# A second batch's scores kept in a copy instead of computed twice, and the order of work around them

## The chip, the cores and the metric

The kernel runs on one core of one Trainium2 chip. A core has TensorE (called PE in the rows: it multiplies, and transposes by multiplying with an identity), VectorE (DVE), ScalarE (ACT), GpSimd (POOL) and SyncE (SP), which issues DMA transfers here. Each engine works through its own list of instructions in order. Products land in PSUM, eight banks of 128 x 512 floats; everything else lives in SBUF. The metric is the time of one execution on the device in microseconds.

## The reference

Eight batches (B) with eight heads (H), 512 tokens (S) of width 64 (D), and 32 states for each head. Tokens read the states and states read the tokens, by one softmax each over the transposed scores. Both results go through one feed-forward layer with a hard gate. In all there are 8 x 544 = 4352 rows of width 512, and 2048 hidden columns.

```
scores = scale * np.matmul(x, state.transpose(0, 1, 3, 2))
a = softmax(scores);  xread = np.matmul(a, state)
scores2 = scale * np.matmul(state, x.transpose(0, 1, 3, 2))
a2 = softmax(scores2); sread = np.matmul(a2, x)
x = concat([xread, sread], axis=2), heads side by side   # 4352 rows
h = x @ w_in
g = h * np.clip(h + 3.0, 0.0, 6.0) / 6.0
return g @ w_out
```

## The kernel before

For the tokens, reading the states and multiplying by w_in are joined: `wprime` makes w' = states x w_in for a batch, and the first product is w' times the softmax weights, turned ("aT"). The hidden columns of a batch are worked in 16 steps of 128, four to a chunk; step n of the program has a first product (`first`, L831, into one of two banks `ps_h`), a gate (ACT L881, DVE L883), a split of the gated values into a high and a low part (ACT L246, DVE L247: `g_hi`, `g_lo`) and, two steps later, a second product into four banks `acc` (`second`, also L831). A product of split numbers is three matmuls. The first four steps work in plain fp32 instead (L860 and L900). In the trace a plain matmul has two records, so an x8 in an order below is an x16 there. The states' own rows come last, as a ninth batch.

Attention of a batch b, in the names of the code:

- `scores_by_columns` (its product is in `all_heads`, L458) multiplies states and tokens into two banks `ps_s`. `tokens_by_columns` makes the tokens' softmax of them (DVE L674 transposes the bank into SBUF; then L565 to L582, L680, and the split `aT_hi`, `aT_lo`). `states` makes the states' softmax of the same scores (DVE max L693, scaling L695, ACT exp L697, reciprocal L700 and L702). For the first two batches the tokens' half is needed early and the states' half is put off: its score product is made once more later (name "L"), so that the two banks are not held meanwhile. The first batch's tokens' half works by rows instead (`tokens_by_rows`), so it needs column scores only once, for the states.
- The states' weights are then laid out for reading: for batch 0 by PE (L731), for batch 1 by a DVE transpose (L745) and 32 small DMAs on SP (L752), for later batches by L758 and 16 DMAs (L766).
- `tokens_read` (64 small matmul records, L796; DVE L805) is the states' reading of the tokens. It rides on a later score product: in one entry with it, right behind. Ahead of its matmuls stands the turn of the result before (L791, one transpose by PE).
- `load_state` fetches the states of a later batch by four DMAs (L382) and turns them on DVE (L389) into `stT`. `load_turned` fetches tokens ahead (L445, sixteen DMAs for a batch), `load_x` the tokens to be read (L413). Weights come by L303; ACT (L308, L312) and DVE (L316, L320, L327) convert them, and w_out is split by ACT L352 and DVE L354. They pass through staging buffers, tag "raw", that the sixteen L445 use later too. Results leave by L935.

The order on each engine is made by a small list scheduler (`Plan`). Each operation is given a cost in us, a rank and what it reads and writes. `T` adds one for PE, `V` for DVE, `S_` for ACT, `Q` for SP; among those that can start about now, the lowest rank goes first. The program is then issued in that order on each engine. The ranks of the early weights, of the second batch and of the put-off halves are a table of numbers near the end (`weights`, `LATE`, `LATE_STEP`, `rank1`).

Of the kernel before, what the change touches and what calls it, by code (L numbers as in the profile page):

```python
# [10 lines left out]
F32 = mybir.dt.float32  # L11
# [3 lines left out]
ALU = mybir.AluOpType  # L15
# [134 lines left out]
def tile_state_attention_then_hardswish_ffn(  # L150
# [218 lines left out]
    def load_state(b, rank, after=()):  # L369
# [15 lines left out]
        if b < TURNED:  # L385
# [3 lines left out]
        V(0.22, rank + 1.0, lambda: nc.vector.transpose(  # L389
            get(("stT", b), lambda: att.tile([P, P], F32, name="stT")), made[key]), [key], [("stT", b)])  # L390
# [84 lines left out]
    def wprime(b, parts, rank, banks=None, after=()):  # L475
# [12 lines left out]
        at = T(0.26 + sum(0.95 * w[3] / CH for w in work), rank, run,  # L488
               [("stT", b)] + [k for c, f0, f1, *_ in work for k in w_in_keys(c * FPC + f0, c * FPC + f1)],
               [k for w in work for k in w[5]], after)  # L490
# [178 lines left out]
    def tokens_by_columns(b, rank, ps):  # L669

        hi_lo = weights_of(b)
        for g in range(NG):
# [12 lines left out]

    def states(b, rank, ps):

        r_key = ("r2", (b, 0))
        r2 = lambda: get(r_key, lambda: small.tile([P, NG], F32, name="r2", bufs=2))
        for g in range(NG):  # L690
# [3 lines left out]
                n2(), bank(ps[g]), axis=AX.X, op=ALU.max), [ps[g]], [n_key])  # L694
# [3 lines left out]
                tmp(e_key), bank(ps[g]), AF.Exp, bias=n2(), scale=SCALE, accum_out=r2()[:, g : g + 1]),  # L698
                [ps[g], n_key], [e_key, (*r_key, g)])
# [75 lines left out]
    def tokens_read(b, tag="ps_s"):  # L775
# [13 lines left out]
        def read():  # L789
            for key in last_key:  # L790
                nc.tensor.transpose(bank(pr)[:, place(1)], tmp(key)[:, : NG * D], ident)  # L791
# [19 lines left out]
        return 1.0 + 0.11 * len(last), read, [*t_key, *x_parts, *last_key], [pr], then  # L811

    def tokens_read_alone(b, rank, after=()):
        cost, read, reads, writes, then = tokens_read(b)
        T(cost + 0.2, rank, read, reads, writes, after)
        then()
# [158 lines left out]
    for seg, (b, c0, c1) in enumerate(segments):  # L975
# [11 lines left out]
        (0, "in", 0, 1, ("early0", 0, 0), -5.67, -19.58), (1, "in", 1, 1, ("early0", 0, 1), -3.50, -8.04),  # L987
        (2, "in", 2, 2, ("early1", 0), 0.77, -7.20), (-0.34, "out", 0, 1, ("raw", ("out", 0)), -2.50, -6.17),
        (-0.90, "out", 1, 1, ("raw", ("out", 1)), -0.36, -1.02), (0.55, "out", 2, 1, ("raw", ("out", 2)), 2.49, -3.00),
        (5.05, "out", 3, 1, ("early3", 0, 0), 2.13, -1.44),  # L990
# [73 lines left out]
    at(6, lambda: [f(4.88 + 0.2 * k) for k, f in enumerate(late_halves)])  # L1064
# [31 lines left out]
    take_in(0, -14.82, (), accs)  # L1096
    tokens_by_rows(0, lambda k: -2.51, lambda k: (), accs)
    load_x(1, -3.76)
    for n in range(len(steps)):
# [7 lines left out]
        elif b < 2 and n % FPC == 0:  # L1107
            ends = wp_parts[b, c][1:] + [FPC]
            for f0, f1 in zip(wp_parts[b, c], ends):
                weights_until(n + f1 - 1)  # L1110
                s = n - 3 + f0
                wprime(b, [(c, f0, f1)], s + 0.41 if n else (11.83, -6.49, 0.01)[f0],
                       ["acc2", "acc3"] if n == 0 and f1 < 3 else None,
                       [first_of[s]] if n >= 8 else ())
        if n == 0:
            take_in(1, -0.41, [scores_at[0]])
# [41 lines left out]
```

## Time and profile before

| | us |
|---|---|
| median of 3 runs | 663.51 (663.09 to 663.54) |
| the profiled execution | 663.73 |
| its span | 661.9 |
| PE busy | 651.0 (98%) |
| DVE busy | 420.2 (63%) |
| ACT busy | 310.8 (47%) |

The span runs from the first to the last thing that the profiler recorded; 1.83 us of the execution's time lie around it. A timeline row has the start, the busy time, engine, line, operation, output and inputs, the tile (rows x columns of PE used), the operand's shape and the number of records; in brackets stand idle time just before it and what ended that. A row of a DMA queue (SPq) gives the time that the queue took to issue, not the landing. A row of windows has the stretch, its length, then busy time and instructions of PE, PE's weight loads, DVE, ACT and POOL, the granted clock, the DMA share and GB/s. One matmul of 512 columns is recorded as busy longer than the distance to the next, so costs are read from start to start.

### The profile page before, as it was taken

The page shows a single profiled execution, that of the slowest core. Times are in us where ns is not written, and L with a number is a line of the kernel's source. Part 1 is how long each engine was busy: PE and PEld are TensorE (multiplying, and loading weights), DVE is VectorE, ACT ScalarE, POOL GpSimd, SP SyncE. Part 2 cuts the span into 40 slices and gives each one's busy share as a digit, 9 for nine tenths or more (in the row PEclk, how much of TensorE's full clock was granted, in tenths as well). Part 3 has the DMA queues.
Part 4 walks back from the last instruction along what each step waited for, and adds up shares of the span by engine and source line. Part 5 has one row for each costly group of instructions (what it writes and reads, how often), then busy time and mean ns, then how long its engine had stood idle before and what let it go on. Part 6 is the DMA issues. An engine that isn't in the chain of part 4 may idle for free.

```text
span 661.9 us, 9937 instructions
## 1 busy us (share of the span) xinstructions
PE 651.0 (98%) x3950; PEld 502.5 (76%) x3950; DVE 420.2 (63%) x697; ACT 310.8 (47%) x520; POOL 1.0 (0%) x7
## 2 busy tenths in 40 slices
PE   8899999999999999999999999999999999999997
PEld 7446777777686877787877877787778788788896
DVE  4998999885846945953677356944585353543542
ACT  5888777543523543443444343633343343333542
POOL 0000000000000000000000000000000000000000
PEclk9999999999999999999999999999999999999999
DMA  9807452415052243314050503132131001000101
GB/s 272 308 0 214 133 181 81 96 27 139 13 109 74 34 70 94 66 26 70 1 132 9 84 5 109 24 52 44 65 65 24 8 1 65 1 0 1 64 0 33
DMA packets 130894, 46.26 MB, mean 70 GB/s; under 512 B 119200, under 2 KB 121248, under 8 KB 130720
## 3 DMA queue, kind: packets, MB, share of 16 engines
q1 hardware_dynamic: 130704, 45.37, 27.9%
q8 instruction: 31, 0.51, 0.3%
q10 hardware_dynamic: 144, 0.26, 0.1%
q14 instruction: 15, 0.12, 0.1%
HBM read 33.03 MB, written 8.91 MB: 63 GB/s over the span
## 4 chain that ended last, share of the span: by engine, by line
PE 92%; DVE 3%; SPq 2%; DMA 2%; issue 0%; ACT 0%; DVEq 0%; ACTq 0%
PE acc L831 53%; PE ps_h L831 28%; PE ps_s L458 4%; PE acc L900 2%; DMA st_raw<-in_state_dram 2%; PE ps_h L458 2%; SPq L752 2%; PE ps_h L796 1%; PE ps_h L860 1%; PE ps_s L611 1%; SPq L382 0%; DVE g L883 0%; PE acc L546 0%; DVE g_lo L247 0%; DVE s L571 0%
## 5 line engine op out<-in xcount | busy, mean ns | idle before, releaser
L831 PE MATMUL acc<-w_out_hi,g_hi 128*128 128x512 f32 x528 | 209.1, 396 | 0.0
L831 PE MATMUL acc<-w_out_hi,g_lo 128*128 128x512 f32 x528 | 205.6, 389 | 0.3 <-DVE g_lo L247 0.3
L831 PE MATMUL acc<-w_out_lo,g_hi 128*128 128x512 f32 x528 | 205.9, 390 | 0.0
L881 ACT ACTIVATE g<-ps_h,three 128x512 f32<-128x512 f32 (+1 forms) x144 | 95.6, 664 | 212.5 <-PE ps_h L831 208.2
L883 DVE SCALAR_TENSOR_TENSOR g<-g,ps_h 128x512 f32<-128x512 f32 (+1 forms) x144 | 94.5, 657 | 136.9 <-ACT g L881 136.2
L831 PEld LDWEIGHTS acc<-w_out_hi,g_hi 128*128 128x128 f32 x528 | 99.1, 188 | 35.5 <-issue 13.4
L246 ACT CAST g_hi<-g 128x512 fp32r<-128x512 f32 (+1 forms) x140 | 83.3, 595 | 85.1 <-DVE g L883 84.8
L247 DVE TENSOR_TENSOR g_lo<-g,g_hi 128x512 fp32r<-128x512 f32 (+1 forms) x140 | 92.0, 657 | 46.2 <-ACT g_hi L246 43.8
L831 PEld LDWEIGHTS acc<-w_out_hi,g_lo 128*128 128x128 f32 x528 | 99.1, 188 | 21.8 <-DVE g_lo L247 0.8
L831 PEld LDWEIGHTS acc<-w_out_lo,g_hi 128*128 128x128 f32 x528 | 99.2, 188 | 18.9
L831 PE MATMUL ps_h<-aT_hi,wp_hi 128*128 128x512 f32 (+1 forms) x248 | 90.7, 366 | 0.0
L831 PE MATMUL ps_h<-aT_hi,wp_lo 128*128 128x512 f32 (+1 forms) x248 | 89.7, 362 | 0.0
L831 PE MATMUL ps_h<-aT_lo,wp_hi 128*128 128x512 f32 (+1 forms) x248 | 89.7, 362 | 0.0
L831 PEld LDWEIGHTS ps_h<-aT_hi,wp_hi 128*128 128x128 f32 x248 | 46.8, 189 | 8.5 <-DVE wp_lo L247 0.3
L831 PEld LDWEIGHTS ps_h<-aT_lo,wp_hi 128*128 128x128 f32 x248 | 46.8, 189 | 8.2 <-DVE early L316 0.3
L831 PEld LDWEIGHTS ps_h<-aT_hi,wp_lo 128*128 128x128 f32 x248 | 46.8, 189 | 7.3
L831 PE MATMUL ps_h<-aT_hi,wp 128*128 128x512 f32 x128 | 44.6, 389 | 0.0
L831 PEld LDWEIGHTS ps_h<-aT_hi,wp 128*128 128x128 f32 x128 | 24.0, 188 | 5.0
L831 PE MATMUL ps_h<-aT_lo,wp 128*128 128x512 f32 x64 | 24.9, 389 | 0.0
L458 PE MATMUL ps_s<-w_in,stT 64*32 64x512 f32 (+1 forms) x384 | 24.0, 557 | 0.0
L537 DVE STREAM_TRANSPOSE tmp<-raw 128x512 f32<-128x512 f32 x24 | 16.4, 699 | 6.5 <-DMA raw<-in_x_dram 6.5
L247 DVE TENSOR_TENSOR wp_lo<-ps_s,wp_hi 128x512 fp32r<-128x512 f32 (+1 forms) x34 | 19.8, 621 | 0.3 <-ACT wp_hi L246 0.3
(119 smaller groups left out, 506.4 us busy)
## 6 DMA issues: line engine op xcount, KB each, us to landing
out_dram<-ot SPq DMA_DIRECT2D x8, 1024.0 KB, 4.5
early<-in_moe_w_in_dram SPq DMA_DIRECT2D x7, 1024.0 KB, 7.1
xb<-in_x_dram SPq DMA_DIRECT2D x28, 256.0 KB, 4.1
raw<-in_x_dram SPq DMA_DIRECT2D x96, 64.0 KB, 2.1
early<-in_moe_w_out_dram SPq DMA_DIRECT2D x4, 1024.0 KB, 5.5
raw<-in_moe_w_out_dram SPq DMA_DIRECT2D x7, 512.0 KB, 4.4
raw<-raw SPq DMA_DIRECT2D x96, 32.0 KB, 2.0
early<-in_moe_w_in_dram SPq DMA_DIRECT2D x2, 512.0 KB, 5.3
```

The costliest lines, as they stand in the source:

```text
L246: S_(cost, rank, lambda: nc.scalar.copy(hi(), src()), reads, [writes[0]])
L247: V(cost, rank, lambda: nc.vector.tensor_tensor(lo(), src(), hi().bitcast(F32), op=ALU.subtract), [*reads, writes[0]], [writes[1]])
L458: nc.tensor.matmul(out[u][cols, :], made["stT", b][rows, cols], moving(q)[rows], start=True, stop=True,)
L537: V(0.7, rank, lambda q=q, key=key: nc.vector.transpose(xT(b, q), made[key][:, q % 2]), [(*key, q % 2, u, k) for u in range(2) for k in ra ...
L611: nc.tensor.matmul(out[:, j, q], xT(b, q)[:, js], apart[:, q], start=True, stop=True,)
L752: nc.sync.dma_start(dst[:, :, q], src[:, :, c])
L796: nc.tensor.matmul(bank(pr)[cols, u * D : (u + 1) * D], e2T(b, u)[:, j * P + q * NS : j * P + (q + 1) * NS], x_tile(b, True)[:, NG * q + u ...
L831: nc.tensor.matmul(ps, l, r, start=start and k == 0, stop=stop and k == n - 1)
L860: nc.tensor.matmul(bank(ps), made["wp_32", (b, k)][:, g, fs], a_first(g), start=g == 0, stop=g == NG - 1)
L881: S_(cost + 0.05, rank, lambda: nc.scalar.activation(g(), bank(ps)[:, :width], AF.Relu, bias=three), [ps], [g_key])
L883: V(cost, rank, lambda: nc.vector.scalar_tensor_tensor(g(), g(), 6.0, bank(ps)[:, :width], op0=ALU.min, op1=ALU.mult), [ps], [g_key])
L900: nc.tensor.matmul(bank(acc), made["g_hi", n][:, js], plain_out[i][1](), start=opens, stop=closes)
```

## The change

- The second score product of batch 1 goes. Right after the first one, ACT copies its two banks into SBUF (`kept_key`, L686 of the new file), and the put-off `states(1)` takes max and exp from the copies. The copies and the DVE transposes (L690) read the same banks; in the new order the transposes wait for ACT.
- `tokens_read(0)`, which rode on that product, now rides on the w' product of step 12.
- Where a score product has a rider, the turn of the last result (`first`, L833) is issued ahead of the scores, no longer between scores and read.
- The DVE transpose of a later batch's states (L393) is its own function, `turn_state`, added six steps after their load.
- The ranks of the early weights, of the first two batches' attention and of the put-off halves are other numbers.

The lines get new numbers: L458 becomes L462, L831 L858, L860 L887, L900 L927, L791 L833, L796 L815, L883 L910, L674 L690, L693 L714, L745 L766, L752 L773, L389 L393, L382 stays, L445 L449.

```diff
@@ load_state
         plan.add("Q", 1.8, rank, load_blocks, (), [key], after, 400.0)
-        V(0.22, rank + 1.0, lambda: nc.vector.transpose(
-            get(("stT", b), lambda: att.tile([P, P], F32, name="stT")), made[key]), [key], [("stT", b)])
+
+    def turn_state(b, rank, after):
+
+        key = ("st_raw", b)
+        V(0.22, rank, lambda: nc.vector.transpose(
+            get(("stT", b), lambda: att.tile([P, P], F32, name="stT")), made[key]), [key], [("stT", b)], after)
@@ wprime
+            for r in riders:
+                r[1]()
...
+        for r in riders:
+            r[4]()
@@ scores_by_columns
-        riders = [tokens_read(b - 1, "ps_h")] if b >= TURNED or name == "L" and b else []
+        riders = [tokens_read(b - 1, "ps_h")] if b >= TURNED else []
 
         def run():
+            for r in riders:
+                r[5]()
             all_heads(b, [bank(k) for k in ps], lambda q: xT(b, q))
-            for _, read, _, _, _ in riders:
-                read()
+            for r in riders:
+                r[1]()
@@ tokens_by_columns
+        if b < TURNED:
+
+            for g in range(NG):
+                S_(0.6, URGENT, lambda g=g: nc.scalar.copy(tmp(kept_key(b, g)), bank(ps[g])),
+                   [ps[g]], [kept_key(b, g)])
@@ states
+        scores_key = lambda g: ps[g] if ps else kept_key(b, g)
+        scores = lambda g: bank(ps[g]) if ps else tmp(kept_key(b, g))
...
-                n2(), bank(ps[g]), axis=AX.X, op=ALU.max), [ps[g]], [n_key])
+                n2(), scores(g), axis=AX.X, op=ALU.max), [scores_key(g)], [n_key])
...
-                tmp(e_key), bank(ps[g]), AF.Exp, bias=n2(), scale=SCALE, accum_out=r2()[:, g : g + 1]),
-                [ps[g], n_key], [e_key, (*r_key, g)])
+                tmp(e_key), scores(g), AF.Exp, bias=n2(), scale=SCALE, accum_out=r2()[:, g : g + 1]),
+                [scores_key(g), n_key], [e_key, (*r_key, g)])
@@ tokens_read
         def read():
-            for key in last_key:
-                nc.tensor.transpose(bank(pr)[:, place(1)], tmp(key)[:, : NG * D], ident)
...
+        def first():
+            for key in last_key:
+                nc.tensor.transpose(bank(pr)[:, place(1)], tmp(key)[:, : NG * D], ident)
@@ the tables
-        (0, "in", 0, 1, ("early0", 0, 0), -5.67, -19.58), (1, "in", 1, 1, ("early0", 0, 1), -3.50, -8.04),
+        (0, "in", 0, 1, ("early0", 0, 0), 16.36, -26.80), (1, "in", 1, 1, ("early0", 0, 1), -6.71, -8.31),
...
-    LATE_TOLD, AGAIN, MOVED = (8, 12), 12.0, 22
-    LATE, LATE_STEP, HALVES = (2.35, 6.00), (0.38, 0.50), 1.45
+    LATE_TOLD, AGAIN, MOVED = (8, 12), 16.0, 22
+    READ_WITH = (12, 0)
+    LATE, LATE_STEP, HALVES = (2.35, 10.97), (0.16, 5.31), 6.21
@@ fetch
+        at(s0 + 7, lambda: turn_state(b, s0 + 6, [first_of[s0 + 6]]))
@@ late
-            states(b, rank, scores_by_columns(b, LATE[b] + 0.01, (), "L"))
+            states(b, rank, None if b else scores_by_columns(b, LATE[b] + 0.01, (), "L"))
```

PE's first rows after the start, before the change (`w_in_187,stT` and `wp` are w' and its use; `w_in_307,stT`, whose tile holds the turned tokens of batch 1, is the score product of batch 1, and `xT,stT` that of batch 0):

```order
L860 MATMUL ps_h<-w_in_322,wp_243 128x512 x4
L458 MATMUL ps_s<-w_in_187,stT 32x256 x8
L900 MATMUL acc_382<-raw,g 128x512
L458 MATMUL ps_s<-w_in_187,stT 32x512 x8
L860 MATMUL ps_h<-w_in_322,wp_243 128x512 x2
L900 MATMUL acc_412<-raw,g 128x512
L458 MATMUL ps_s<-w_in_307,stT 32x512 x8
L900 MATMUL acc_432<-raw,g 128x512
L900 MATMUL acc_437<-raw,g 128x512
L458 MATMUL ps_s<-xT,stT 32x512 x8
L860 MATMUL ps_h<-w_in_322,wp_243 128x512 x2
```

And after it:

```order
L887 MATMUL ps_h<-w_in_322,wp_243 128x512 x2
L462 MATMUL ps_s<-w_in_187,stT 32x256 x8
L887 MATMUL ps_h<-w_in_322,wp_243 128x512 x2
L462 MATMUL ps_s<-w_in_187,stT 32x512 x8
L887 MATMUL ps_h<-w_in_322,wp_243 128x512 x2
L927 MATMUL acc_403<-raw,g 128x512
L462 MATMUL ps_s<-xT,stT 32x512 x8
L927 MATMUL acc_422<-raw,g 128x512
L927 MATMUL acc_428<-raw,g 128x512
L927 MATMUL acc_436<-raw,g 128x512
L887 MATMUL ps_h<-w_in_322,wp_243 128x512 x2
L462 MATMUL ps_s<-w_in_307,stT 32x512 x8
```

The first of the second products (L900, now L927) stands further back, and the scores of batch 1 come after those of batch 0.

DVE's rows around step 20, where the staging buffer of the sixteen token loads comes free (the first L354 of raw) and batch 1's weights are moved (L745), before the change:

```order
L354 TENSOR_TENSOR w_out_lo_1206<-raw,w_out_hi_1202 128x512
L247 TENSOR_TENSOR g_lo<-g,g_hi 128x512
L320 SCALAR_TENSOR_TENSOR raw<-raw 128x512
L327 SCALAR_TENSOR_TENSOR raw<-raw 128x512
L883 SCALAR_TENSOR_TENSOR g<-g,ps_h 128x512
L354 TENSOR_TENSOR w_out_lo_1206<-raw,w_out_hi_1202 128x512
L247 TENSOR_TENSOR g_lo<-g,g_hi 128x512
L247 TENSOR_TENSOR wp_lo<-ps_s,wp_hi 128x512 x2
L745 STREAM_TRANSPOSE tmp<-tmp 128x512
L883 SCALAR_TENSOR_TENSOR g<-g,ps_h 128x512
L745 STREAM_TRANSPOSE tmp<-tmp 128x512
```

And after it:

```order
L320 SCALAR_TENSOR_TENSOR raw<-raw 128x512
L327 SCALAR_TENSOR_TENSOR raw<-raw 128x512
L714 TENSOR_REDUCE nm_1243<-tmp 128x1
L910 SCALAR_TENSOR_TENSOR g<-g,ps_h 128x512
L354 TENSOR_TENSOR w_out_lo_1195<-raw,w_out_hi_1186 128x512
L247 TENSOR_TENSOR wp_lo<-ps_s,wp_hi 128x512
L247 TENSOR_TENSOR g_lo<-g,g_hi 128x512
L247 TENSOR_TENSOR wp_lo<-ps_s,wp_hi 128x512
L716 TENSOR_SCALAR nm_1243<-nm_1243 128x1
L714 TENSOR_REDUCE nm_1287<-tmp 128x1
L716 TENSOR_SCALAR nm_1287<-nm_1287 128x1
L766 STREAM_TRANSPOSE tmp<-tmp 128x512
```

The two reductions of batch 1's states, which stood near step 9, now stand here, right ahead of the transpose; two earlier L354 of raw stand ahead of the first row shown.

PE's rows at the score product of batch 2, before the change:

```order
L831 MATMUL ps_h<-aT_hi,wp_lo 128x512
L458 MATMUL ps_s<-tmp,stT 32x512 x8
L791 MATMUL ps_h<-ident,tmp 128x128
L796 MATMUL ps_h<-xb,tmp 32x64 x32
L831 MATMUL acc_1479<-w_out_hi_1101,g_hi 128x512
```

And after it:

```order
L858 MATMUL ps_h<-aT_hi,wp_lo 128x512
L833 MATMUL ps_h<-ident,tmp 128x128
L462 MATMUL ps_s<-tmp,stT 32x512 x8
L815 MATMUL ps_h<-xb,tmp 32x64 x32
L858 MATMUL acc_1473<-w_out_hi_1105,g_hi 128x512
```

The turn has changed places with the scores, and the same holds at the score products of the five later batches.

On DVE the state's transpose of batch 3, which stood between the two L674 of batch 2 and a g_lo, stands after the change behind the whole softmax of batch 2, some gates further on.

More of the change, by code (lines that the diff above doesn't have):

```diff
@@ L473, in wp_of, with wprime @@
         return get((f"wp_{half}", (b, c)), lambda: gp.tile([P, NG, CH], F32R, name=f"wp_{half}"))
-    def wprime(b, parts, rank, banks=None, after=()):
+    def wprime(b, parts, rank, banks=None, after=(), riders=()):
         banks = banks or ["ps_s", "ps_s", "ps_h", "ps_h"]
@@ L486, in run @@
                 all_heads(b, [bank(k)[:, :n] for k in bs], lambda q: w_in_of(c)[:, q, fs])
-        at = T(0.26 + sum(0.95 * w[3] / CH for w in work), rank, run,
-               [("stT", b)] + [k for c, f0, f1, *_ in work for k in w_in_keys(c * FPC + f0, c * FPC + f1)],
-               [k for w in work for k in w[5]], after)
+            for r in riders:
+                r[1]()
+        at = T(0.26 + sum(0.95 * w[3] / CH for w in work) + sum(r[0] for r in riders), rank, run,
+               [("stT", b)] + [k for c, f0, f1, *_ in work for k in w_in_keys(c * FPC + f0, c * FPC + f1)]
+               + [k for r in riders for k in r[2]],
+               [k for w in work for k in w[5]] + [k for r in riders for k in r[3]], after)
+        for r in riders:
+            r[4]()
         for c, f0, _, n, fs, bs in work[::-1]:
@@ L810, in then, with run @@
                 put(c, pr, place(1))
-        return 1.0 + 0.11 * len(last), read, [*t_key, *x_parts, *last_key], [pr], then
+        def first():
+            for key in last_key:
+                nc.tensor.transpose(bank(pr)[:, place(1)], tmp(key)[:, : NG * D], ident)
+        return 1.0 + 0.11 * len(last), read, [*t_key, *x_parts, *last_key], [pr], then, first
     def tokens_read_alone(b, rank, after=()):
-        cost, read, reads, writes, then = tokens_read(b)
-        T(cost + 0.2, rank, read, reads, writes, after)
+        cost, read, reads, writes, then, turn_last = tokens_read(b)
+        def run():
+            turn_last()
+            read()
+        T(cost + 0.2, rank, run, reads, writes, after)
         then()
@@ L1095, in tile_state_attention_then_hardswish_ffn @@
     accs = [f"acc{q}" for q in range(NQ)]
-    take_in(0, -14.82, (), accs)
+    take_in(0, -14.56, (), accs)
     tokens_by_rows(0, lambda k: -2.51, lambda k: (), accs)
```

21 lines of the change are left out of this document (12 added, 9 removed).

## The prediction

> **What bounds the kernel now.** I read the page first: busy time, then the chain of waits, then the busy time in windows.
>
> ```profile
> span 661.9 us, 9937 instructions
> PE 651.0 (98%) x3950; PEld 502.5 (76%) x3950; DVE 420.2 (63%) x697; ACT 310.8 (47%) x520; POOL 1.0 (0%) x7
> PE 92%; DVE 3%; SPq 2%; DMA 2%; issue 0%; ACT 0%; DVEq 0%; ACTq 0%
> 60.00:120.00 60.00, 60.00 (x372) 46.09 (x361) 56.20 (x81) 45.30 (x67) 0.00 (x0) 1.00 0.45 133
> 150.00:172.00 22.00, 21.66 (x184) 14.60 (x183) 15.63 (x32) 8.58 (x17) 0.00 (x0) 1.00 0.40 103
> 172.00:662.00 490.00, 485.20 (x2888) 385.65 (x2886) 276.04 (x462) 197.74 (x337) 0.00 (x0) 1.00 0.21 45
> ```
>
> TensorE (PE) is busy for 98% of the span and makes up 92% of the chain. The clock column is 1.00 in every window. In the last window PE is busy for 485.20 of 490 us, and the rest of that is the last result's way out after the last product. So the end can come sooner in two ways only: PE gets less to do, or it stops waiting before 172 us. VectorE (DVE) is not the bound over the span, but between 60 and 120 us it is busy for 56.20 of 60 us, so there a late DVE instruction stays late. The other small shares of the chain, DVE, SP's queue and DMA, must be short stretches before 172 us. The timelines show where.
>
> **The change part by part.** First, the second score product of the second batch (b=1).
>
> ```profile
> 58.26 0.40 PE L831 MATMUL acc<-w_out_hi,g_lo 128*128 128x512 f32 x1
> 58.58 1.09 PE L458 MATMUL ps_s<-w_in,stT 64*32 64x512 f32 x16
> 59.60 1.10 PE L796 MATMUL ps_h<-xb,tmp 128*32 128x64 f32 x64
> 60.63 0.50 PE L831 MATMUL acc<-w_out_hi,g_hi 128*128 128x512 f32 x1
> 60.97 0.39 PE L831 MATMUL acc<-w_out_lo,g_hi 128*128 128x512 f32 x1
> 550.96 0.39 PE L831 MATMUL ps_h<-aT_hi,wp_lo 128*128 128x512 f32 x1
> 551.19 0.27 PE L791 MATMUL ps_s<-ident,tmp 128*128 128x128 f32 x1
> 551.39 1.10 PE L796 MATMUL ps_s<-xb,raw 128*32 128x64 f32 x64
> ```
>
> I cost blocks from start to next start, since the ends are modelled. The 16 records at 58.58 take 59.60 - 58.58 = 1.02 us. Going in costs 58.58 - 58.26 = 0.32 where the usual step is 551.19 - 550.96 = 0.23, and coming out costs 60.97 - 60.63 = 0.34. That is 0.09 and 0.11 more. The first batch's read (L796, after the change L815), which rode on this block, now rides on a product of states and w_in that PE makes anyway (step 12). It takes its 1.03 us there and no extra turn in and out. So PE saves 1.02 + 0.09 + 0.11 = **1.2 us of work**.
>
> The copies that replace the product are two of 128x512 on ACT. ACT is busy for 47% of the span. The max and exp of those scores read the copy instead of the bank, as many instructions as before.
>
> Second, the start.
>
> ```profile
> 23.85 0.62 ACT L551 COPY w_in<-ps_s 128x512 f32<-128x512 f32 x1
> 29.00 1.17 PE L900 MATMUL acc<-raw,g 128*128 128x512 f32 x2 [1.29 <-DVE g L883]
> 33.92 1.09 PE L458 MATMUL ps_s<-w_in,stT 64*32 64x512 f32 x16
> 34.95 2.07 PE L900 MATMUL acc<-raw,g 128*128 128x512 f32 x4
> 36.94 1.09 PE L458 MATMUL ps_s<-xT,stT 64*32 64x512 f32 x16
> 37.96 1.98 PE L860 MATMUL ps_h<-w_in,wp 128*128 128x512 f32 x4
> 39.78 6.47 PE L900 MATMUL acc<-raw,g 128*128 128x512 f32 x14
> 35.11 1.31 DVE L674 STREAM_TRANSPOSE tmp<-ps_s 128x512 f32<-128x512 f32 x2 [0.30 <-PE ps_s L458]
> 44.06 1.28 DVE L247 TENSOR_TENSOR aT_lo<-tmp,aT_hi 128x512 fp32r<-128x512 f32 x2
> 45.66 0.81 PE L831 MATMUL ps_h<-aT_hi,wp_hi 128*128 128x512 f32 x1
> ```
>
> At 29.00 PE waits 1.29 us for DVE's gate. The new order puts the first second-product (L900, now L927) behind two more of the first products and one more block of w', so the gate is done by then: **1.3 us** less waiting. The second batch's own scores (33.92) move later, though. Ahead of them now stand one more pair of first products (39.78 - 37.96 = 1.8), four more records of second products (36.94 - 34.95 = 2.0) and the first batch's column scores (37.96 - 36.94 = 1.0), less the 1.3: 3.5 us later. The chain from there to the second batch's turned weights took from 35.11 to the end of 44.06 + 1.28. An ACT copy now goes ahead of each DVE transpose, some 0.6 by the 23.85 row. So the two halves of aT_lo end at about 45.3 + 3.5 + 0.6 = 49.4, give or take half a microsecond. The new order also moves PE's first use of them later: fifteen second-product rows, that is thirty records at 39.78's pace of (45.66 - 39.78) / 14 = 0.42, then come before it, which puts that use near 49.4 too. I take no loss; the bounds are 0 and 1.2 (rival B).
>
> The rule that speaks against this copy is in the Trainium skill, "PSUM — Partial Sum Buffer", section "PSUM bank collisions raise a hardware error": ScalarE and VectorE must not read one bank in the same quadrant at once. If it holds here, copy and transpose go one after the other, as the DVE transpose waiting for ACT in the new order does; the sum by it has the 0.6 in the chain, without it aT_lo would be ready 0.6 sooner and rival B would all but vanish. No run here shows what happens when both read at once.
>
> Third, from 60 to 155 us, the queue ahead of the second batch's read.
>
> ```profile
> 66.13 0.69 DVE L693 TENSOR_REDUCE nm<-ps_s 128x1 f32<-128x512 f32 x1
> 120.41 0.68 DVE L354 TENSOR_TENSOR w_out_lo<-raw,w_out_hi 128x512 fp32r<-128x512 f32 x1
> 129.08 0.70 DVE L745 STREAM_TRANSPOSE tmp<-tmp 128x512 f32<-128x512 f32 x1
> 121.12 8.30 SPq L445 DMA_DIRECT2D raw<-in_x_dram  x16
> 130.08 22.14 SPq L752 DMA_DIRECT2D tmp<-tmp  x32
> 152.90 2.99 SPq L382 DMA_DIRECT2D st_raw<-in_state_dram  x4
> 153.29 1.27 PE L796 MATMUL ps_h<-xb,tmp 128*32 128x64 f32 x64
> ```
>
> With 1.2 + 1.3 saved, and 0.15 from the turn (below), PE comes to the read at 153.29 about 2.65 sooner. But this read was already late: it took 1.27 where the others take 1.10, waiting for the last of 32 small DMAs (L752), which SP issued for 22.14 us. SP began those once it had issued sixteen L445, and these began when DVE had freed a staging buffer (the L354 at 120.41). So the read moves only as far as that L354 does. In the new order the batch's two max reductions (66.13, 0.69 each: some 1.4 us of a saturated DVE) stand behind that L354 and not ahead of it, and PE's own 2.5 us feeds the gates earlier. I put L354 1.4 to 2.5 us sooner, and with it the queue. The DVE transpose that opens the L752 (L745, now L766) must come sooner as well; in the new order it follows the two reductions and two exps directly and would end near 127.7, when SP is ready near 128. So I take **2.2 us** at this point, out of 1.4 to 2.8 (PE's whole 2.65 and the 0.17 of waiting).
>
> Fourth, the state's turn.
>
> ```profile
> 159.19 0.31 DVE L389 STREAM_TRANSPOSE stT<-st_raw 128x128 f32<-128x128 f32 x1 [2.85 <-DMA st_raw<-in_state_dram]
> 168.69 0.67 DVE L883 SCALAR_TENSOR_TENSOR g<-g,ps_h 128x512 f32<-128x512 f32 x1
> 165.28 0.39 PE L831 MATMUL acc<-w_out_hi,g_lo 128*128 128x512 f32 x1
> 166.74 0.50 PE L831 MATMUL acc<-w_out_hi,g_lo 128*128 128x512 f32 x1 [0.33 <-DVE g_lo L247]
> 167.86 1.09 PE L458 MATMUL ps_s<-w_in,stT 64*32 64x512 f32 x16
> 168.74 1.75 PE L458 MATMUL ps_h<-w_in,stT 64*32 64x512 f32 x16
> 202.29 1.06 PE L458 MATMUL ps_h<-w_in,stT 64*32 64x512 f32 x16
> ```
>
> The state's DMA is issued at 152.90, behind those 32, and DVE stands at the head of its queue for it for 2.85 us. Behind it stand g_lo, the third batch's softmax and the gates. PE pays twice. From 165.28 to 167.86 it issues seven matmuls, which at 0.23, with 0.32 into the block, is 1.70; it took 2.58, so 0.9 lost. And the second block of w' at 168.74, which needs the bank that the gate at 168.69 frees, shows 1.75 where 202.29 shows 1.06: 0.7 lost. The change puts this transpose six steps later, behind that softmax, where the DMA has long landed; w' of the next batch is its first reader, far behind. All of it back would be 1.6; since DVE keeps the softmax in the same place, only sooner, I take **1.4**, bounds 0.7 (one of the two losses stays) and 1.6.
>
> Fifth, the turn of the last result.
>
> ```profile
> 210.65 0.33 PE L791 MATMUL ps_h<-ident,tmp 128*128 128x128 f32 x1
> 210.91 1.10 PE L796 MATMUL ps_h<-xb,raw 128*32 128x64 f32 x64
> ```
>
> Between scores and read the turn costs 210.91 - 210.65 = 0.26 and, since L458 to L796 needs no more, nothing else goes. Ahead of the scores it follows an L831, as at 551.19, at the usual 0.23, and the next block starts 0.20 behind (551.39). Before: 0.32 in, 1.02, 0.26, so 1.60 from the last L831 to the read. Now: 0.23 + 0.20 + 1.02 = 1.45, or 1.54 if the 0.09 of going into small tiles is still paid. That is 0.06 to 0.15 for each; six batches have it, one is within the third part, and five give **0.7**, bounds 0.3 and 0.75. The result to be turned is an older one and PE does not wait for it now, so asking for it a microsecond sooner should be covered.
>
> The other ranks move loads and weight splits; the loads are the same ones. I put them at nothing, bounds -0.5 and +0.5, the sizes of one wait like that of 166.74.
>
> Sum: 2.2 + 1.4 + 0.7 = 4.3 us. The profiled execution took 663.73, 0.22 above the median of 663.51; its span is 661.9 and 1.83 lie around it. 663.73 - 4.3 = 659.4, or **659.2** by the median, which I forecast. Bounds of the terms: 1.4 + 0.7 + 0.3 - 0.5 = 1.9, and 2.8 + 1.6 + 0.75 + 0.5 = 5.65.
>
> **The rivals.**
> A: the queue does not move. If DVE does the L354 at 120.41 no sooner, then the 32 DMAs land when they did, the read ends when it did, and the 2.65 before it turns into a longer wait there. Gained are the fourth and fifth parts only: 1.4 + 0.7 = 2.1, so 661.4. For it: DVE is at 56.20 of 60. Against: the 1.4 us of reductions that leave the stretch.
> B: the wait at 29.00 comes back near 49 us. If copies, transposes and softmax take 1 us longer than I reckon, PE stands before the first aT_lo for up to 1.2 and the third part shrinks to 1.2 or so: about 660.4. For it: both times fall on 49.4. Against: the queue caps the same gain, so most of such a loss would not be seen at the end.
> C, the other side: the moved batch's weights come too late. Its max, exp and transpose are now the lowest in rank, while 22.14 us of SP issues hang on them. The read ends at 153.29 + 1.27 = 154.6, the first L745 at 129.08 + 0.70 = 129.8. With 2.1 gained behind it, the kernel is slower once that transpose ends later than 129.8 + 2.1 = 131.9, since the queue behind it moves with it; at 134.5 it would be 663.51 + 2.6 = 666.1. For it: the reductions stand behind four gates in DVE's order. Against: exp needs only ACT, which is half idle, and the order puts the transpose in the place where it stood.
> D: the change doesn't do what it says, in that PE still waits as before for the state's turn, since the same softmax delays it: 663.51 - 2.2 - 0.7 = 660.6.
>
> **How the numbers follow.** Forecast 0.52, A 0.2, B 0.09, C 0.06, D 0.13. The range takes in the upper bound of the sum on one side (663.51 - 5.2 = 658.3) and A with half a microsecond on the other: 658.3 to 661.9, in which I see eight of ten. A measurement of this kernel tells about 0.2%, 1.33 us, so faster means below 662.2. All cases but C and the bad tail of A lie there: faster 0.88, same 0.07, slower 0.05.
>
> **What would show it.** No L458 block at 58 us and no wait at 29 us; PE's first use of aT_lo without idle time; the sixteen L445 starting near 119 and the 32 moves near 128; PE's read of b=1 starting near 151; no DVE wait for st_raw near 157, and the w' block behind it at 1.06. I would be wrong if the L445 still began at 121, if the new L766 ended after 130, or if PE showed a new wait between 60 and 125 us, where DVE has no slack for a later g_lo.

## The result, and the profile after

The changed kernel takes 659.88 us (median of 4 runs, 659.53 to 660.24) where the kernel before took 663.30 (median of 4, 663.06 to 663.54): a ratio of 0.9937, interval 0.9915 to 0.9958, so 3.4 us or 0.5% less. The forecast was 659.2. Two later sessions gave 659.62 and 659.68, with ratios of 0.9937 (0.9925 to 0.9950) and 0.9941 (0.9928 to 0.9953).

The page of the profiled execution, which took 660.08 us: its span, busy time, and the chain of waits by engine and by line.

```profile
span 658.2 us, 9905 instructions
PE 647.7 (98%) x3934; PEld 502.1 (76%) x3934; DVE 420.4 (64%) x697; ACT 312.1 (47%) x522; POOL 1.0 (0%) x7
PE 89%; SPq 6%; DMA 2%; DVE 1%; issue 1%; ACT 0%; DVEq 0%; ACTq 0%
...
172.00:662.00 490.00, 481.36 (x2873) 382.81 (x2871) 272.39 (x457) 195.57 (x333) 0.00 (x0) 1.00 0.21 45
```

PE has 3.3 us less to show as busy, and its share of the chain fell from 92% to 89%, while SP's queue rose from 2% to 6%. Less of the time is set by PE's work, more by the issuing of DMAs. The timelines of PE and then of SP's queue show where.

```profile
31.19 1.06 PE L927 MATMUL acc<-raw,g 128*128 128x512 f32 x2
...
49.30 0.81 PE L858 MATMUL ps_h<-aT_hi,wp_hi 128*128 128x512 f32 x1
149.80 0.27 PE L833 MATMUL ps_h<-ident,tmp 128*128 128x128 f32 x1
150.00 1.09 PE L462 MATMUL ps_s<-tmp,stT 64*32 64x512 f32 x16
151.02 0.82 PE L815 MATMUL ps_h<-xb,tmp 128*32 128x64 f32 x38
152.21 0.61 PE L815 MATMUL ps_h<-xb,tmp 128*32 128x64 f32 x26 [0.37 <-DMA tmp<-tmp]
166.09 1.06 PE L462 MATMUL ps_h<-w_in,stT 64*32 64x512 f32 x16
196.61 0.50 PE L858 MATMUL acc<-w_out_hi,g_lo 128*128 128x512 f32 x1
```

```profile
119.63 8.99 SPq L449 DMA_DIRECT2D raw<-in_x_dram  x16
129.25 21.59 SPq L773 DMA_DIRECT2D tmp<-tmp  x32
150.94 0.54 SPq L962 DMA_DIRECT2D out_dram<-ot  x1
151.52 2.98 SPq L382 DMA_DIRECT2D st_raw<-in_state_dram  x4
172.93 11.53 SPq L787 DMA_DIRECT2D raw<-raw  x16
184.51 8.57 SPq L449 DMA_DIRECT2D raw<-in_x_dram  x16
```

No product of scores stands at 58 us, and the wait at 29.00 is gone. The w' block at 166.09 is back to 1.06 from 1.75. Two places are left: the second batch's read breaks in two at 152.21, where PE waits for the last of the 32 moves, and at 196.61 PE comes late to a g_lo. The table has the start of the first matmul behind each place (from the same timelines); the third column is the first of the two repeats (`e1`), the last a version from the end of the experiments (`e11`).

| behind | before | after | again | e11 |
|---|---|---|---|---|
| the start-up: first product | 23.51 | 24.03 | 23.43 | 23.52 |
| the second batch's read | 154.49 | 152.74 | 152.45 | 151.68 |
| the third batch's w' | 170.43 | 167.08 | 166.80 | 166.03 |
| the next w' | 203.29 | 200.30 | 199.74 | 198.73 |
| the last score block: last read starts | 551.39 | 547.69 | 547.14 | 546.12 |
| span | 661.9 | 658.2 | 657.7 | 656.7 |

Before against again: 2.0 us is won by the read, 1.6 more by w', nothing up to the next w', 0.7 more by the last read. That is a span shorter by 4.2.

### The profile page after: what moved, and what is told of

Same layout as the page of the kernel before. It is cut to its first block, busy times and chain, and to the rows that moved or that the text cites. A ratio compares the mean times of both kernels' runs of the same rounds, so it can differ in the third digit from the quotient of the medians.

```text
span 658.2 us, 9905 instructions
## 1 busy us (share of the span) xinstructions
PE 647.7 (98%) x3934; PEld 502.1 (76%) x3934; DVE 420.4 (64%) x697; ACT 312.1 (47%) x522; POOL 1.0 (0%) x7
## 4 chain that ended last, share of the span: by engine, by line
PE 89%; SPq 6%; DMA 2%; DVE 1%; issue 1%; ACT 0%; DVEq 0%; ACTq 0%
PE acc L858 51%; PE ps_h L858 27%; PE ps_s L462 4%; SPq L773 2%; PE acc L927 2%; SPq L787 2%; PE ps_h L462 2%; SPq L449 1%; PE ps_h L887 1%; PE ps_h L815 1%; DMA ot<-in_x_dram 1%; DMA tmp<-tmp 1%; PE ps_s L620 1%; DMA st_raw<-in_state_dram 0%; DMA raw<-in_x_dram 0%
## 5 line engine op out<-in xcount | busy, mean ns | idle before, releaser
L858 PE MATMUL acc<-w_out_hi,g_hi 128*128 128x512 f32 x528 | 208.9, 396 | 0.0
L858 PE MATMUL acc<-w_out_lo,g_hi 128*128 128x512 f32 x528 | 205.9, 390 | 0.0
L858 PE MATMUL acc<-w_out_hi,g_lo 128*128 128x512 f32 x528 | 205.7, 390 | 0.1
L910 DVE SCALAR_TENSOR_TENSOR g<-g,ps_h 128x512 f32<-128x512 f32 (+1 forms) x144 | 94.6, 657 | 134.6 <-ACT g L908 133.3
L858 PEld LDWEIGHTS acc<-w_out_hi,g_hi 128*128 128x128 f32 x528 | 99.1, 188 | 34.0 <-issue 11.3
L858 PEld LDWEIGHTS acc<-w_out_hi,g_lo 128*128 128x128 f32 x528 | 99.1, 188 | 21.5 <-DVE g_lo L247 0.6
L858 PEld LDWEIGHTS acc<-w_out_lo,g_hi 128*128 128x128 f32 x528 | 99.2, 188 | 19.1
L858 PE MATMUL ps_h<-aT_hi,wp_hi 128*128 128x512 f32 (+1 forms) x248 | 90.6, 365 | 0.0
L858 PE MATMUL ps_h<-aT_hi,wp_lo 128*128 128x512 f32 (+1 forms) x248 | 89.8, 362 | 0.0
L858 PE MATMUL ps_h<-aT_lo,wp_hi 128*128 128x512 f32 (+1 forms) x248 | 89.7, 362 | 0.0
L858 PEld LDWEIGHTS ps_h<-aT_hi,wp_hi 128*128 128x128 f32 x248 | 46.8, 189 | 8.5 <-DVE g L910 0.5
L858 PEld LDWEIGHTS ps_h<-aT_lo,wp_hi 128*128 128x128 f32 x248 | 46.8, 189 | 8.2 <-issue 0.5
L858 PEld LDWEIGHTS ps_h<-aT_hi,wp_lo 128*128 128x128 f32 x248 | 46.8, 189 | 7.2
L858 PE MATMUL ps_h<-aT_hi,wp 128*128 128x512 f32 x128 | 44.6, 389 | 0.0
L858 PEld LDWEIGHTS ps_h<-aT_hi,wp 128*128 128x128 f32 x128 | 24.0, 188 | 5.0
L858 PE MATMUL ps_h<-aT_lo,wp 128*128 128x512 f32 x64 | 24.9, 389 | 0.0
L462 PE MATMUL ps_s<-w_in,stT 64*32 64x512 f32 (+1 forms) x368 | 22.9, 555 | 0.0
```

What stands on the lines that cost most here:

```text
L462: nc.tensor.matmul(out[u][cols, :], made["stT", b][rows, cols], moving(q)[rows], start=True, stop=True,)
L858: nc.tensor.matmul(ps, l, r, start=start and k == 0, stop=stop and k == n - 1)
L910: V(cost, rank, lambda: nc.vector.scalar_tensor_tensor(g(), g(), 6.0, bank(ps)[:, :width], op0=ALU.min, op1=ALU.mult), [ps], [g_key])
```

## The experiments

The theory from the trace: between 120 and 152 us the list of DMAs on SP sets the time, not PE's work; DVE's wait for the states was worth 1.6; the turn 0.7. The rival: PE's work sets the time all along, so that 1.2 us of product is 1.2 us of time.

**The same kernel again (e1, and e12 in a later session).** No edit.

> The changed kernel itself, once more, as the one to compare the next three with and to see which of its small losses come back. Theory: 659.9 us again; its PE waits for the last of the 32 moves at the second batch's read (0.58 us lost at 152.2 in the first profile) and for a late g_lo at 196.6 (0.30 and 0.11 lost). If the 0.5 us by which its first product started later than before (24.03 against 23.51) is a difference of the runs and not of the order, the first product starts near 23.5 here and the time is as much shorter.

659.62 us. The first product starts at 23.43, so the half microsecond at the start was a difference of runs. PE lost more at the read: from its start to the next product it took 2.03 us, where the first profile took 1.72 and e11 below, which has no wait there, takes 1.17. Near 196 PE lost 0.2, where the first profile lost 0.4. In the last session:

> The changed kernel once more, to compare with the run before it on the same chip: 659.6 to 659.9. Its first product starts near 23.5; the read of the second batch waits 0.6 to 0.9 for the last moves.

659.68 us, first product at 23.41. The read took 1.93, so it lost 0.76, and at 196 PE lost 0.6. The loss at 196 is larger where SP took longer for the sixteen moves (L787) ahead of it: 11.5 us in the first profile and 11.4 here, 11.2 in e1, and 11.0 in e4 below, which lost 0.1. Some of those moves took much longer to issue than the rest (last section).

**The turn between scores and read (e2).**

```diff
         def run():
-            for r in riders:
-                r[5]()
             all_heads(b, [bank(k) for k in ps], lambda q: xT(b, q))
             for r in riders:
+                r[5]()
+            for r in riders:
                 r[1]()
```

> The changed kernel with the turn of the last result between scores and read again, as before; nothing else moves. Theory: 0.14 us dearer at each of the five later reads, and nothing at the second batch's, where the queue of moves sets the end: 0.7 more, 660.6. Rival (it costs at all six): 0.86 more. Rival (the turn is hidden either way): no change, 659.9.

660.38 against 659.62 in the same session: 0.76 more, as the theory has it. The five runs spread from 659.50 to 661.17, so the medians alone do not tell 0.7 from the 0.86 of the first rival. The traces do: the second batch's read is left at 152.40, against 152.45 in e1, so nothing is lost there, and the last read starts 0.75 later (547.89 against 547.14). At the third batch's read the rows are these, first of this run and then of the changed kernel:

```profile
207.16 0.33 PE L833 MATMUL ps_h<-ident,tmp 128*128 128x128 f32 x1
207.41 1.10 PE L815 MATMUL ps_h<-xb,raw 128*32 128x64 f32 x64
```

```profile
206.33 0.39 PE L858 MATMUL ps_h<-aT_hi,wp_lo 128*128 128x512 f32 x1
206.56 0.27 PE L833 MATMUL ps_h<-ident,tmp 128*128 128x128 f32 x1
206.76 1.09 PE L462 MATMUL ps_s<-tmp,stT 64*32 64x512 f32 x16
207.78 1.10 PE L815 MATMUL ps_h<-xb,raw 128*32 128x64 f32 x64
```

From the last L858 to the read the changed kernel takes 1.45 us, to the hundredth what the prediction put for it.

**The state's transpose early again (e3).** In the issued list one DVE instruction, the transpose of the fourth batch's states, goes back behind the two score transposes of the third.

```diff
+        row = self.order()
+        for group, anchor in self.moved:
+            for n in group:
+                row.remove(n)
+            at = row.index(anchor) + 1
+            row[at:at] = group
...
+    plan.moved = [([plan.turned[b]], plan.cut[b - 1]) for b in (3,)]
```

> The changed kernel with one DVE instruction put back: the transpose of the fourth batch's states stands right behind the two score transposes of the third, as before. Theory: DVE waits there for the DMA of the states, PE loses the 1.6 us near 163 to 168 again, less the 0.4 that it now loses at 196.6 for another reason: 1.2 to 1.6 more, 661.1 to 661.5. Rival (the rest of the new order has freed that place too): under 0.4 more.

661.78: 2.2 more, above the 1.2 to 1.6 of the theory. DVE waits and PE loses what they did before, 0.9 ahead of w' and 0.7 in it:

```profile
157.20 0.31 DVE L403 STREAM_TRANSPOSE stT<-st_raw 128x128 f32<-128x128 f32 x1 [2.89 <-DMA st_raw<-in_state_dram]
```

```profile
164.74 0.50 PE L869 MATMUL acc<-w_out_hi,g_lo 128*128 128x512 f32 x1 [0.33 <-DVE g_lo L257]
166.75 1.75 PE L472 MATMUL ps_h<-w_in,stT 64*32 64x512 f32 x16
```

The other 0.4 is lost up to the next w', where PE also loses 0.4 to a late g_lo at 198; e1 lost 0.2 at this place. The rival, that the new order had freed this place too, falls.

**The product put back (e4).**

```diff
+    def scores_again():
+        ps = [bank(("ps_s", ("L", 1, u))) for u in range(NG)]
+        all_heads(1, ps, lambda q: xT(1, q))
...
                 self.ops[n][3]()
+                if n == self.behind:
+                    self.extra()
...
+    plan.behind, plan.extra = first_of[7], scores_again
```

> The changed kernel with the second batch's score product made once more by PE near 60 us, its result unused; every other instruction stays in its place. PE has 1.2 us more work there. Theory (from 120 to 152 us SP's queue of DMAs sets the time, and PE waits 0.58 at its end): 0.6 is absorbed at 152 and up to 0.4 at 196, so 0.2 to 0.6 more, 660.1 to 660.5, with no PE wait left at 152. Rival (PE's work sets the time all along): 1.2 more, 661.1.

660.12: 0.5 more by the medians, not 1.2. The rows of PE at the read, this run first and then the changed kernel again (e1):

```profile
59.04 1.09 PE L464 MATMUL ps_s<-w_in,stT 64*32 64x512 f32 x16
...
151.54 1.25 PE L817 MATMUL ps_h<-xb,tmp 128*32 128x64 f32 x64
152.72 0.50 PE L860 MATMUL acc<-w_out_hi,g_hi 128*128 128x512 f32 x1
```

```profile
150.42 1.12 PE L815 MATMUL ps_h<-xb,tmp 128*32 128x64 f32 x38
151.91 0.61 PE L815 MATMUL ps_h<-xb,tmp 128*32 128x64 f32 x26 [0.37 <-DMA tmp<-tmp]
152.45 0.50 PE L858 MATMUL acc<-w_out_hi,g_hi 128*128 128x512 f32 x1
```

PE comes 1.1 later to the read and leaves it 0.3 later; the wait is what gives. Not all of this is the queue's fixed end: the loads began 1.1 later here, and the queue still ended at 150.64, since it had fewer long single issues (31.6 us from the first load to the next store in e1, 30.5 here). By the next w' the trace has 0.14 left (199.88 against 199.74).

**The copies alone, in the kernel before (e5).** The second product goes, the copies come, every other instruction stays.

```diff
+            def keep_and_turn(g=g, bt_key=bt_key):
+                if b < TURNED:
+                    nc.scalar.copy(tmp(("tmp", ("kept", b, g))), bank(ps[g]))
+                nc.vector.transpose(tmp(bt_key), bank(ps[g]))
...
-            all_heads(b, [bank(k) for k in ps], lambda q: xT(b, q))
+            if name == "C" or not b:
+                all_heads(b, [bank(k) for k in ps], lambda q: xT(b, q))
```

> The kernel before, with one part of the change alone: the second batch's second score product is gone, and ACT's two copies feed its max and exp; every other instruction stays in its place. PE has 1.2 us less work near 58 us. Theory (SP's queue of DMAs sets the time of the second batch's read, and of the states' load behind it): PE waits that much longer there and the end moves by 0 to 0.3, 663.2 to 663.5. Rival (work taken from PE is time gained): 1.2 less, 662.3.

664.80, a ratio of 1.0016 (1.0007 to 1.0025): the change's main part, alone, makes the kernel a little slower. The rival falls, but the theory has missed something too. ACT, DVE and PE near 36 us:

```profile
35.22 0.57 ACT L677 COPY tmp<-ps_s 128x512 f32<-128x512 f32 x1
36.25 0.58 ACT L677 COPY tmp<-ps_s 128x512 f32<-128x512 f32 x1
```

```profile
35.83 0.72 DVE L678 STREAM_TRANSPOSE tmp<-ps_s 128x512 f32<-128x512 f32 x1 [1.15 <-ACT tmp L677]
36.86 0.72 DVE L678 STREAM_TRANSPOSE tmp<-ps_s 128x512 f32<-128x512 f32 x1 [0.31 <-ACT tmp L677]
```

```profile
36.82 1.90 PE L458 MATMUL ps_s<-xT,stT 64*32 64x512 f32 x16
```

Each transpose starts when the copy of its bank has ended, so the banks are held about a microsecond longer, and the next score product, which needs them, takes 1.90 where it took 1.09. The product saves 1.0 us here, not 1.2, since the rider stays in its place with its turn in and out. Of that, 0.8 is lost on the spot; part of that is the place of the second copy, behind a cast (e10 has the copies next to each other and loses 0.15). The rest vanished in the waits at 153 and 166: behind w' PE is where it was (170.41 against 170.43). The next w' ends 0.3 later, behind a late g_lo near 200, and that is all the trace shows of the 1.1 by which the median rose. The rule on bank collisions in the Trainium skill, "PSUM — Partial Sum Buffer", section "PSUM bank collisions raise a hardware error", is what these waits keep to. They show its price here; whether the chip would fault without them was not tried.

**The states' transposes late, in the kernel before (e6).** The same kind of move as in e3, the other way, for five batches: each transpose goes behind the last split of the softmax ahead of it.

```diff
+    plan.moved = [([plan.turned[b]], plan.cut[b - 1]) for b in range(3, B)]
```

> The kernel before, with another part alone: the DVE transposes of the later batches' states stand further back, behind the softmax ahead of them, by five moves in DVE's list and nothing else. Theory: the 2.85 us of DVE waiting at 159 and the 1.6 us that PE lost behind it go: 1.6 to 2.0 less, 661.5 to 661.9. Rival (another late instruction takes its place at 166): under 0.8 less.

661.97 against 663.72, ratio 0.9973 (0.9964 to 0.9983): 1.75 less, within the theory. The read still ends at 154.46; the w' block behind it is at 1.06 and 0.9 us sooner, and PE is through with it 1.6 sooner (168.81 against 170.43). The rival falls.

```profile
167.81 1.06 PE L468 MATMUL ps_h<-w_in,stT 64*32 64x512 f32 x16
```

**The maxima early (e7).** In the changed kernel the second batch's max, scaling, exp and reciprocal go back behind the first product of step 9.

```diff
+    plan.moved = [(plan.group, first_of[9])]
```

> The changed kernel with the second batch's max, scaling, exp and reciprocal put back near step 9, as before; on PE and SP nothing moves. 1.4 us of DVE work goes ahead of the split (L354) that frees the staging buffer of the sixteen token loads. Theory (SP's queue starts with that buffer and sets the read): the loads start 1.3 later, and the time is 0.9 to 1.4 more, 660.5 to 661.0. Rival (the queue's end does not hang on its start, as the run with the product back suggests, where the loads began 1.1 later and the queue still ended at 150.6): 0 to 0.3 more, 659.6 to 659.9.

660.26, ratio 0.9948 (0.9936 to 0.9961), where the changed kernel has 0.9937 and 0.9941: 0.5 to 0.7 more, between the two. Against e1 the loads start at 119.84 instead of 119.03, so 0.8 later and not 1.3, and the read ends at 153.03 instead of 152.45. DVE had slack for the other 0.5: for 0.32 of it, it stands idle in e1 at 115.97, waiting for ACT, and not in e7.

**Four of the 32 moves on ACT's queue (e8),** planned anew.

```diff
-                            nc.sync.dma_start(dst[:, :, q], src[:, :, c])
+                            (nc.scalar if g and c == 3 else nc.sync).dma_start(dst[:, :, q], src[:, :, c])
```

> The changed kernel with the last four of the 32 moves issued by ACT's queue and not by SP's: SP has 2.6 us less to issue before the second batch's read, ACT some 2.4 us more near 131. Theory (the read waits for the last move): its 0.9 us of waiting goes and nothing takes its place, 0.6 to 0.9 less, 658.7 to 659.0. Rival (ACT then delivers its gates late, or the read waits for something else): no gain or worse, 659.6 or more.

659.01, ratio 0.9930 (0.9917 to 0.9943): about 0.5 less than the changed kernel. The read's wait is gone, it ends 0.9 sooner (151.55), but at 193 to 196 PE loses 0.8, where e1 lost 0.2. There DVE stands before tokens that SP loads behind the third batch's sixteen moves, which shows in the changed kernel's own rows too:

```profile
193.02 0.71 DVE L546 STREAM_TRANSPOSE tmp<-raw 128x512 f32<-128x512 f32 x1 [1.20 <-DMA raw<-in_x_dram]
...
195.27 0.71 DVE L546 STREAM_TRANSPOSE tmp<-raw 128x512 f32<-128x512 f32 x1 [0.97 <-DMA raw<-in_x_dram]
195.91 0.65 DVE L247 TENSOR_TENSOR g_lo<-g,g_hi 128x512 fp32r<-128x512 f32 x1
```

**Four of those sixteen there too (e9),** planned anew.

```diff
-                    nc.sync.dma_start(dst[:, :, q], src[:, :, c])
+                    (nc.scalar if b == 2 and c == 3 else nc.sync).dma_start(dst[:, :, q], src[:, :, c])
```

> The run with the split moves, and the last four of the third batch's sixteen moves (near 180 us) on ACT's queue too, so that SP comes sooner to the sixteen token loads for which DVE stood waiting there (195). Theory (in the run with the split moves PE lost 0.6 at 193 to 196 behind that wait): all of it comes back, and PE waits for nothing after 23 us: 0.4 to 0.6 less than that run, 658.4 to 658.6. Rival (the four issues hold up ACT's gates and splits there, 2.4 us of ACT in a stretch where PE needs them): no gain or worse, 659.0 or more.

661.05, 2.0 more than e8: the theory fails. The planner had put a result's addition on DVE behind two of those token transposes, and PE waited for its bank:

```profile
188.18 0.50 PE L864 MATMUL acc<-w_out_hi,g_hi 128*128 128x512 f32 x1 [2.15 <-DVE ot L953]
```

The profiled execution took 662.56. Behind this wait, from 188 to 193 us, the granted clock in it is 0.66, and eight matmuls start 0.43 apart instead of 0.23: another 1.6 lost. What the runs near the median lost that way is not known.

**The start's old ranks (e10),** in the changed kernel, planned anew.

```diff
-        (0, "in", 0, 1, ("early0", 0, 0), 16.36, -26.80), (1, "in", 1, 1, ("early0", 0, 1), -6.71, -8.31),
+        (0, "in", 0, 1, ("early0", 0, 0), -5.67, -19.58), (1, "in", 1, 1, ("early0", 0, 1), -3.50, -8.04),
...
-            rank1 = lambda k: (-0.81, 4.10, 1.92, 0.14, 0.41)[k]
-            tokens_by_columns(1, rank1, scores_by_columns(1, 3.10, [wp_at[0, 0, 2]]))
+            rank1 = lambda k: (1.71, 2.50, 1.58, -2.06, 0.41)[k]
+            tokens_by_columns(1, rank1, scores_by_columns(1, 1.99, [wp_at[0, 0, 2]]))
```

> The changed kernel with the ranks of the early weights, of the first w' and of the second batch's attention from before, and so planned anew: the first second-product stands at its old place behind the first w', and the second batch's scores ahead of the first batch's again. Theory: the 1.3 us wait at 29 comes back, and the first batch's scores wait 0.8 for banks that the copies still read, as in the kernel before with the copies alone; up to 0.9 of these 2.1 vanishes in the waiting at the second batch's read, so 0.8 to 2.1 more than the changed kernel, 660.5 to 661.8. Rival (the queue absorbs nearly all, as it did with the product put back): under 0.5 more.

660.68, ratio 0.9954 (0.9942 to 0.9967), about 1.0 more.

```profile
28.97 1.17 PE L927 MATMUL acc<-raw,g 128*128 128x512 f32 x2 [1.33 <-DVE g L910]
36.92 1.24 PE L462 MATMUL ps_s<-xT,stT 64*32 64x512 f32 x16
```

The wait at 29 is back, but the hold of the banks costs 0.15 here, not 0.8, since the planner sets the two copies next to each other. PE reaches the read 1.6 later than in e1 (152.01 against 150.42) and leaves it 1.1 later (153.58): a third is absorbed.

**Eight moves on ACT's queue, in place (e11).** As e9, but the issued list is the changed kernel's: only the eight moves leave SP's list, four for the place behind the second L766 in the issued list, four for one behind the gate near 184.

```diff
+            plan.moved.append((list(range(len(plan.ops) - 4, len(plan.ops))), first_move - 1))
...
+    plan.moved.append((plan.late_four, plan.gate_of[34]))
```

> Eight moves on ACT's queue as in the run before, but with the order kept: on PE and DVE every instruction stands where the changed kernel has it; on ACT the second batch's last four moves come behind its second transpose (near 130) and the third batch's last four behind a gate near 184, in a stretch where ACT otherwise idles; SP only loses the eight. Theory (the run before lost 2.3 us to the new place of a result's addition in DVE's list, not to the moves): the waiting at the second batch's read (0.9) and the one at 196 go and nothing takes their place: 0.6 to 1.1 less than the changed kernel on the same chip, 658.6 to 659.1. Rival (issues on ACT's queue cost PE time wherever they stand): no gain or worse.

658.67 (658.60 to 658.81) against 659.68 (659.55 to 660.00) of the changed kernel in the same session: 1.0 less, the quickest of all, ratio to the kernel before 0.9925 (0.9912 to 0.9939). PE's timeline shows no idle time from 23 us to its last product; the read takes its plain time. Its last move was issued at 147.30, some three microseconds before it began:

```profile
150.51 1.25 PE L829 MATMUL ps_h<-xb,tmp 128*32 128x64 f32 x64
151.68 0.50 PE L872 MATMUL acc<-w_out_hi,g_hi 128*128 128x512 f32 x1
```

The Trainium skill, "DMA: Bandwidth & Descriptors", section "Issuing engines are not separate DMA queues", says that issuing from several engines saves only the sequencer's issue time, usually small beside the transfer. The first half agrees with the trace: SP is through with 28 moves in 19.38 us where 32 took 21.59, and the four that ACT issues land no sooner (2.1 us from issue to landing, 1.8 on SP). The second does not fit it: a move takes 0.60 us to issue and 1.8 to land, and 32 of them in one list are 21.6 us, so that moving eight was worth a microsecond.

## Why the prediction was right

The sum was 4.3 us; the medians differ by 3.4, 3.9 and 3.9, the spans by 3.7 and 4.2. So the forecast of 659.2 was 0.4 to 0.7 too low. The lower end of the range was reckoned with 5.2 us, though the bounds of the terms add up to 5.65, which would be 657.9; the result lies above both.

- **The product, 1.2 us of work.** Right in size (e4: PE 1.1 later at the read), and right that it is not time by itself: put back it costs 0.5, taken out alone it gains nothing (e5). That the copies stand in the sum with nothing, beside a remark that ACT has room, was wrong as a step: their price is on PE, by way of the banks that they hold (0.8 in e5, 0.15 in e10). In the new order the first batch's scores stand ahead of the second's, and no row shows that price.
- **The start, 1.3 us.** The wait is gone (no idle time ahead of 31.19, the new place of the first second-product), and e10 puts its worth, with the order around it, at about 1.0. The first use of the second batch's weights at 49.30 comes without a wait, so rival B falls.
- **The read, 2.2 us.** Measured 1.75, or 2.04 in the repeat. The start of the queue was named rightly: the loads begin with the first L354 of raw, which ends the staging buffer's use (118.92 + 0.68 in the row below). They came 1.5 to 2.1 sooner (119.63 and 119.03 against 121.12), inside the 1.4 to 2.5. Put back one at a time, the two reductions cost the loads 0.8 (e7) and PE's product 1.1 (e4). Rival A, that the queue does not move, falls, but the queue did take back 0.6 to 0.9 of what PE had won.
- **The wait at the read before, 0.17 us.** This reading was wrong. The read's 1.27 was no wait for the last move: e11 takes 1.25 with all moves long landed. (What makes it longer than the 1.10 of the other reads was not traced.) The rows below are from the chains of waits (start, length, what), the first before the change, the next three after it; the last row is DVE's, after the change. Before, the last move was issued at 151.62 and had landed some 1.83 later, at 153.45. The second half of the read, 26 records, can start 0.14 behind the landing and is left 0.53 after it starts (152.74 - 152.21). Before, it so started at 154.49 - 0.53 = 153.96, which is 0.37 later than the queue allowed.

```profile
151.62 0.60 SPq L752
```

```profile
150.24 1.83 DMA tmp<-tmp
152.07 0.14 issue
152.21 0.61 PE ps_h L815 x26
```

```profile
118.92 0.68 DVE L354 TENSOR_TENSOR w_out_lo<-raw,w_out_hi 128x512 fp32r<-128x512 f32 x1
```

So PE's work still set the read before the change, by 0.37, and the queue sets it after. The landing came 153.45 - 152.07 = 1.38 sooner, and 1.38 + 0.37 = 1.75 is what the read won. In the repeat, with the landing at 151.78, it is 1.67 + 0.37 = 2.04. Here luck helped: the queue's end won up to 0.4 less than its start, and the slack that the prediction did not see made up for it.

- **The state's turn, 1.4 us.** The term was a little small: all 1.6 came back. e3 and e6 price it at 1.75 to 2.2 with what follows. In the new order DVE turns the state at 174.94 without a wait, so rival D falls.
- **The turn of the result, 0.7 us.** 0.76 in e2, 0.70 between the last two places of the table.
- **The other ranks, nothing.** Here a loss stood that the prediction had only as a bound: 0.2 to 0.6 at 196 in three profiles. Once PE is 3 us ahead, the tokens that SP loads near 190 are late.
- **Rival C, the moved batch's weights too late.** The transpose L766 began at 127.81, and SP was through with the loads and a weight only at 129.15 (128.74 + 0.41): it was in time.

```profile
127.81 0.71 DVE L766 STREAM_TRANSPOSE tmp<-tmp 128x512 f32<-128x512 f32 x1
128.74 0.41 SPq L303 DMA_DIRECT2D raw<-in_moe_w_out_dram  x1
```

So the number came out near with errors that partly cancel: the state's turn was worth 0.2 more, the read 0.2 to 0.4 less, and the queue's second stop, near 196, was missing.

## What to carry to other kernels

When an engine is busy for 98% of the time, work taken from it can still be worth less than its length if a list of DMA issues further on sets the time (1.2 us of product were 0.5 of time in e4): add up the issue times in that list, and look at what starts it. A block that takes longer than its like is not waiting by that alone: set the landing of its last input beside the start of the part that uses it. A copy out of a bank is not free because its engine is idle: it holds the bank, and the next product that needs the bank pays. And where a planner sets the order, a change of one operation is best tried with the rest of the list held fixed; e9 and e11 differ by 2.4 us for the same eight moves.

## What was not expected of the hardware

Single DMA issues on SP, of a kind that takes 0.60 us, took 0.99 to 1.74 at a few places, and not at the same instruction in every run (rows of the chains of waits):

```profile
142.94 1.56 SPq L752
```

```profile
144.71 0.99 SPq L773
178.15 1.74 SPq L787
```

The first is from the kernel before, the others are from the changed one. The whole list from the first token load to the next store took 31.2 us before, 31.3 after, 31.6 in e1 and 30.5 in e4. What holds these issues up was not found. How much of what differs between two executions of the same kernel near 150 and 196 us hangs on it was not separated.
